# One attention-and-mixers kernel: how the first head pair is loaded, rounded and marked, and who copies six PSUM tiles of the first three periods

## The chip, the cores and the metric

The kernel runs on one core of one Trainium2 chip. The metric is device time in microseconds (us) of one execution, in which the kernel reads everything from HBM, computes and writes its output back. The engines are named as in the profile: PE (TensorE, matrix products), PEld (its weight loads), DVE (VectorE), ACT (ScalarE), POOL (GpSimd) and SP (SyncE, which here only starts transfers). Each engine works through its own list of instructions in order and waits for the others by semaphores.

## What is computed

Three layers follow each other. The first is an attention whose mask is a hash: each query and each key gets six sign bits by a projection, and a query sees only the keys with the same six bits. The other two are mixers of large matrix products. Cut to what matters:

```python
q_bits = einsum('bhsd,dk->bhsk', q, proj) > 0     # q, k, v: batch 2, 8 heads, 768 rows, 64 columns
k_bits = einsum('bhsd,dk->bhsk', k, proj) > 0     # proj: 64 x 6
mask   = bucket(q_bits)[..., None] == bucket(k_bits)[..., None, :]
scores = where(mask, q @ k.T / 8, -1e9)
attn   = softmax(scores) @ v                      # then (2, 768, 512)
x      = sigmoid(xr @ w_r) * (relu(xk @ w_k)**2 @ w_v)     # xk, xr: mixes of x and the row before it
u, v   = split(relu(x @ w_in)); v = normalise(v)
out    = (u * (w_spatial @ v + b_spatial)) @ w_out
```

Products are formed from rounded parts: a float32 value is split into a rounded high part and the remainder, the low part, and the low parts are multiplied too.

## The kernel before

The 16 heads are worked on as eight pairs, and each pair as 24 units: a unit is one block of 128 queries of one head against all 768 keys. Three units make a period, so there are 64 periods (`p` in the loop at L518), eight per pair. The units of a pair run over the first half of its queries for head `e` = 0, then for `e` = 1, then over the second half in the same way. So period 0 is head 0, period 1 is head 1, period 2 is head 0 again.

For each head there is one operand tile `TK` of 128 partitions by four slots of 768 columns. One half of the partitions, `lo_rows`, holds the rounded k in slot 0, the low part of k in slot 1, the rounded q in slot 2 and the low part of q in slot 3. The other half, `hi_rows`, holds the rounded k in slot 0, the rounded q in slot 3, and in slots 1 and 2 zeros with twelve rows of scaled sign bits, which make the mask. The scores of a unit (`scores`, L316) are two products with two column halves each, four matmuls: slot 3 against slot 0, then slot 2 against slot 1. The second pair of matmuls therefore needs the bits and the low part of k, and the first needs the low part of q.

A unit then goes through these steps: `peak` (L332) is one pass of DVE that copies the scores out of PSUM and finds their maximum; `bias` is a small scaling on DVE; `expo` (L347) is the exponential on ACT; `transp` (L359) makes six PE transposes in two halves into PSUM tiles `t`; `evac` (L367) copies each half out into `PT` on ACT; and three periods later `av` (L397) multiplies by v. There are two PSUM tiles for scores and three for `t`. So a period has six evictions, all on ACT.

The preparation of a pair has these steps. `load_x` (L236) brings q and k, in float32, into the tile `raw`, of which there is one buffer: the pool has `bufs=1` and each pair takes the tag "x" again, so the load of the next pair waits for the last reader of this one. `load_pair` (L241) brings the rounded parts into `TK` by four transfers from POOL's queue that round on the way. `bits_mm` (L271) is four products of `raw` with the projection, into a `t` tile called `z`; `bits_sign` (L280, DVE) makes the tile `zb` of signs, `bits_scale` (L287) the scaled tile `zc`, and `bits_place` (L292) brings its rows to `TK` by eight small transfers on SP's queue, or, for the first head of the first pair, four by copies on DVE and ACT. `split_part` and `split_piece` (L254 to L263) subtract the rounded part from `raw` to get the low parts.

Jobs of a period are kept in a table `plan` with two places per period: place 0 is after the exponential of the second unit, place 1 at the end of the period. Place 0 of period 0 holds the load of `raw` for pair 1 and `load_pair(1)`; place 0 of period 1 holds `bits_mm(1)`, `bits_sign(1)` and `bits_scale(1)`; periods 1 and 2 hold the eight pieces of the low parts of pair 1 on POOL; and from period 2 on weight conversions run on DVE (L44, L49 and others), with `recip` (L377) in every second period.

Ahead of the loop stands the prologue, L483 to L505, in which the first pair is prepared. `warm` (L265) is a run of PE products on nothing, 12 ahead of the first bits and 8 behind them, each of which shows as two passes in the trace.

Of the kernel before, what the change touches and what calls it, by code (L numbers as in the profile page):

```python
# [10 lines left out]
F32 = mybir.dt.float32  # L11
F32R = mybir.dt.float32r
AF = mybir.ActivationFunctionType
ALU = mybir.AluOpType
AX = mybir.AxisListType

B, H, S, D = 2, 8, 768, 64
NP = H // 2
HS = S // 2
# [1 line left out]
DF = 1024  # L21
NB = 6
BIG = float(2 ** 30)
WARM_A, WARM_B = 12, 8
U32 = mybir.dt.uint32
W_MIN = float(np.array([0x38000000], np.uint32).view(np.float32)[0])
W_MAX = float(np.array([0x47EFFFFF], np.uint32).view(np.float32)[0])
# [55 lines left out]
def hash_attention_moe_kernel(  # L83
# [134 lines left out]
    with tc.manual_schedule():  # L218
        attention(**env)
        mixers(**env)  # L220


def attention(tc, nc, mid, dram, ident, msc, omu, misc, cst_sb, pb, epsT, kq, vP, XT, TK0, wr, w_r, wk,
              w_k, w_v, ps_s, ps_t, obank, mix_jobs, r_group, tick, now, at_tick, plan_weight, wv, **_):
    PS = bass.MemoryType.PSUM
    with ExitStack() as ctx:
        at = ctx.enter_context(tc.tile_pool(name="at", bufs=1))

        TK = [TK0, [at.tile([128, 4, S], F32R, name=f"tk1_{e}") for e in range(2)]]
        lo_rows = {0: slice(64, 128), 1: slice(0, 64)}  # L230
        hi_rows = {0: slice(0, 64), 1: slice(64, 128)}

        raw, vt = {}, {}
        npairs = B * NP

        def load_x(pp):  # L236
            b, p = divmod(pp, NP)
            raw[pp] = mid.tile([128, 2, S], F32, tag="x", name="x")
            (nc.gpsimd if pp > 1 else nc.sync).dma_start(raw[pp], kq[b, p].rearrange("t r s -> r t s"))

        def load_pair(pp):  # L241
            b, p = divmod(pp, NP)
            for e in range(2):
                src = kq[b, p][:, 64 * (1 - e):64 * (1 - e) + 64].rearrange("t d s -> d t s")
                t = TK[pp % 2][e]
                nc.gpsimd.dma_start(t[lo_rows[e], 0:3:2, :], src)
                nc.gpsimd.dma_start(t[hi_rows[e], 0:4:3, :], src)

        def load_v(pp):
            b, p = divmod(pp, NP)  # L250
            vt[pp] = at.tile([128, 6, 2, D], F32, tag="v", bufs=2, name="v")
            nc.sync.dma_start(vt[pp], vP[b, p])
# [7 lines left out]
        def split_part(pp, e, n, eng):  # L260
            l = lo_rows[e]
            t = TK[pp % 2][e]
            eng.tensor_sub(t[l, 1 + 2 * n, :], raw[pp][l, n], t[l, 2 * n, :])  # L263

        def warm(n):  # L265
            for _ in range(n):
                nc.tensor.matmul(obank[:, :128], ident, ident, start=True, stop=True)

        zs = {}

        def bits_mm(pp):  # L271
            zs[pp] = ps_t.tile([128, 512], F32, tag="t", name="z")
            for g in range(4):
                o = (g % 2) * HS
                nc.tensor.matmul(
                    zs[pp][32 * g:32 * g + 32, :HS], pb, raw[pp][:, 1 - g // 2, o:o + HS],
                    start=True, stop=True,
                )

        def bits_sign(pp):  # L280
            zb = at.tile([128, HS], F32, tag="zb", name="zb")
            nc.vector.tensor_scalar(
                zb, zs[pp][:, :HS], 0.0, cst_sb[:, 0:1], op0=ALU.is_gt, op1=ALU.subtract
            )
            zs[pp] = zb

        def bits_scale(pp, eng):  # L287
            zc = at.tile([128, HS], F32R, tag="zc", name="zc")
            eng.tensor_scalar(zc, zs[pp], cst_sb[:, 1:2], None, op0=ALU.mult)
            zs[pp] = zc  # L290

        def bits_place(pp, first=False):  # L292
            zc = zs.pop(pp)
            for e in range(2):
                for g in range(4):
                    o = (g % 2) * HS
                    a0 = 64 * e
                    s0 = 32 * g + 12 * e
                    dst = TK[pp % 2][e][a0:a0 + 12, 2 - g // 2, o:o + HS]
                    src = zc[s0:s0 + 12, :].bitcast(F32)  # L300
                    if first and e == 0:
                        if g % 2:
                            nc.vector.tensor_copy(dst, src)
                        else:
                            nc.scalar.copy(dst, src)
                    else:
                        nc.sync.dma_start(dst.bitcast(F32), src)

        def clear(r, eng):
            for e in range(2):  # L310
                eng.memset(TK[r][e][hi_rows[e], 1:3, :].bitcast(F32), 0.0)
# [4 lines left out]
        def scores(i):  # L316
            g, u = divmod(i, 6)
            pp, half = divmod(g, 2)
            e, j = divmod(u, 3)
            t = TK[pp % 2][e]  # L320
            q0 = half * HS + 128 * j
            s = ps_s.tile([128, 2, 512], F32, tag="s", name="s")
            for n in range(2):
                w = t[:, 3 - n, q0:q0 + 128]
                for c in range(2):
                    nc.tensor.matmul(  # L326
                        s[:, c, :HS], w, t[:, n, c * HS:(c + 1) * HS],
                        start=(n == 0), stop=(n == 1),
                    )
            S_ps[i] = s  # L330

        def peak(i):  # L332
            s = S_ps.pop(i)
            c = at.tile([128, 2, HS], F32, tag="p", bufs=3, name="p")
            m = at.tile([128, 1], F32, tag="m", bufs=4, name="m")
            nc.vector.tensor_scalar(  # L336
                c, s[:, :, :HS], -BIG / 2, None, op0=ALU.max, op1=ALU.max, accum_out=m
            )
            C_sb[i] = (c, m)

        def bias(i):
            c, m = C_sb[i]
            nb = at.tile([128, 1], F32, tag="nb", bufs=4, name="nb")
            nc.vector.tensor_scalar(nb, m, -0.125, None, op0=ALU.mult)  # L344
            C_sb[i] = (c, nb)
# [13 lines left out]
        def transp(i, c):  # L359
            p = P[i] if c == 0 else P.pop(i)  # L360
            t = ps_t.tile([128, 512], F32, tag="t", name="t")
            for n in range(3):
                k0 = 128 * (3 * c + n)
                nc.tensor.transpose(t[:, 128 * n:128 * n + 128], p[:, k0:k0 + 128], ident)  # L364
            return t

        def evac(i, c, t):  # L367
            g, u = divmod(i, 6)
            e, j = divmod(u, 3)
            nc.scalar.copy(  # L370
                PT[g][:, e, 3 * c:3 * c + 3, 128 * j:128 * j + 128],
                t[:, :HS].rearrange("p (n q) -> p n q", n=3),
            )
# [43 lines left out]
        plan = {}  # L417
# [3 lines left out]
        def at_slot(p, k, job):  # L421
            plan.setdefault((p, k), []).append(job)
# [58 lines left out]
                at_slot(max(p0 + 3, 0), 0, lambda n=pp + 2: load_x(n))  # L481

        nc.scalar.dma_start(msc, misc)  # L483
        nc.vector.memset(ident, 0.0)
        load_x(0)
        load_pair(0)
        clear(0, nc.vector)
        warm(WARM_A)
        split_part(0, 0, 1, nc.gpsimd)
        split_part(0, 0, 0, nc.vector)  # L490
        bits_mm(0)
        bits_sign(0)
        bits_scale(0, nc.vector)
        bits_place(0, True)
        warm(WARM_B)
        for r in rcs:
            nc.vector.memset(r, 0.0)
        split_part(0, 1, 0, nc.vector)
        split_part(0, 1, 1, nc.gpsimd)
        make_identity(nc, ident)  # L500
        load_v(0)
        nc.gpsimd.memset(XT[:, :, :, 0:1], 0.0)
        nc.gpsimd.memset(epsT, 1e-6)
        nc.gpsimd.tensor_scalar(omu, msc[:, 34:42], -1.0, 1.0, op0=ALU.mult, op1=ALU.add)
        clear(1, nc.gpsimd)  # L505

        def av3(p):
            for n in range(3):
                av(p // 2, 3 * (p % 2) + n)

        def move(i, c):
            evac(i, c, transp(i, c))

        def score(i):
            peak(i)
            bias(i)

        for p in range(np3):  # L518
            a = 3 * p
            scores(a)  # L520
            scores(a + 1)
            score(a)
            if a:
                move(a - 1, 0)
            expo(a)
            if a:
                move(a - 1, 1)
            score(a + 1)
            expo(a + 1)
            if p >= 3:  # L530
                av3(p - 3)
            if p >= 2 and p % 2 == 0:
                recip(p // 2 - 1)
            for job in plan.pop((p, 0), ()):
                job()
            if p >= 3 and p % 2:
                spread((p - 3) // 2)
            if p >= np3 - 2:
                tick()
            scores(a + 2)  # L540
            move(a, 0)
            move(a, 1)
            score(a + 2)
            expo(a + 2)
            if p >= 4 and p % 2 == 0:
                finish((p - 4) // 2)
            move(a + 1, 0)
            move(a + 1, 1)
            for job in plan.pop((p, 1), ()):
                job()  # L550
            if p == np3 - 2:
                plan_wv()
            if p >= np3 - 2:
                tick()
# [322 lines left out]
```

## Time and profile before

| | us |
|---|---|
| median of 3 runs | 560.82 |
| lowest and highest | 560.57, 561.64 |
| span of the profiled execution | 557.4 |
| PE busy in it | 543.7 |
| first matmul of the scores starts | 10.27 |
| `bits_mm` of pair 1 starts | 19.25 |

The profiled execution's span runs from its first to its last instruction. The median lies 3.4 us above it, which is what lies around the instructions. PE is busy for 98% of the span and is the bound from the middle of the first pair on. The stretch that concerns the change is the first 32 us, in which PE is not yet full.

### The profile page before, as it was taken

How to read it: one execution, taken by the hardware profiler on the slowest of the kernel's cores; microseconds unless marked ns; L12 is line 12 of the kernel's file. 1: busy time of each engine (PE TensorE's matmuls, PEld its weight loads, DVE VectorE, ACT ScalarE, POOL GpSimd, SP SyncE). 2: the span in 40 equal slices, each digit the busy share in tenths (PEclk: the TensorE clock that was granted, in tenths of full speed). 3: DMA queues.
4: the chain of work that ended last, by engine and by line, in shares of the span. 5: the costliest groups of instructions: out<-in, count | busy, mean ns of one | idle time of the engine just before them, and what ended most of it. 6: DMA issues, size and time to landing. Idle time of an engine off the chain costs nothing.

```text
span 557.4 us, 9008 instructions
## 1 busy us (share of the span) xinstructions
PE 543.7 (98%) x3188; PEld 465.8 (84%) x3188; DVE 381.4 (68%) x812; ACT 335.4 (60%) x718; POOL 146.4 (26%) x152
## 2 busy tenths in 40 slices
PE   7899999999999999999999999999999999999997
PEld 6767676767676767789999999999998989899896
DVE  6778888888888889558796676316997784443230
ACT  1978888888888879849743856519345443221211
POOL 5774858585858533200000000000110000000000
PEclk9999999999999999999999999999999999999999
DMA  8957494859585710210031211000672100001102
GB/s 175 274 173 150 139 173 147 169 135 180 152 162 167 150 48 16 88 56 7 32 114 39 61 53 39 0 1 2 197 227 85 58 29 2 1 19 39 56 20 95
DMA packets 20477, 51.96 MB, mean 93 GB/s; under 512 B 3840, under 2 KB 6864, under 8 KB 20432
## 3 DMA queue, kind: packets, MB, share of 16 engines
q1 hardware_dynamic: 13664, 31.44, 18.3%
q0 software_dynamic: 6336, 19.66, 17.6%
q8 instruction: 25, 0.41, 0.3%
q10 hardware_dynamic: 432, 0.28, 0.2%
q14 instruction: 20, 0.16, 0.1%
HBM read 47.08 MB, written 3.19 MB: 90 GB/s over the span
## 4 chain that ended last, share of the span: by engine, by line
PE 78%; DVE 13%; ACT 5%; issue 2%; DMA 1%; DVEq 0%; ACTq 0%; POOLq 0%
PE o L176 11%; PE v L631 9%; PE o L399 9%; PE t L364 9%; PE s L326 8%; PE k L176 8%; PE s L176 7%; PE w L176 5%; PE u L176 5%; DVE p L336 5%; PE o L631 3%; PE r L176 3%; ACT p L354 2%; DVE w_a L49 2%; DVE w_a L44 2%
## 5 line engine op out<-in xcount | busy, mean ns | idle before, releaser
L336 DVE TENSOR_SCALAR_CACHE_REDUCE p<-s 128x768 f32<-128x768 f32 x96 | 91.7, 956 | 22.3 <-PE s L326 20.4
L354 ACT ACTIVATE p<-p,nb 128x768 f32<-128x768 f32 x96 | 90.8, 946 | 16.0 <-DVE nb L344 15.4
L370 ACT COPY PT<-t 128x384 f32<-128x384 f32 x192 | 84.1, 476 | 19.3 <-PE t L364 18.5
L326 PE MATMUL s<-tk 128*128 128x384 f32 x384 | 87.1, 360 | 3.8 <-DVE p L336 1.7
L326 PEld LDWEIGHTS s<-tk 128*128 128x128 f32 x384 | 64.7, 191 | 25.0 <-issue 6.7
L364 PE MATMUL t<-ident,p 128*128 128x128 f32 x576 | 78.7, 277 | 3.8 <-ACT p L354 3.8
L364 PEld LDWEIGHTS t<-ident,p 128*128 128x128 f32 x576 | 65.4, 141 | 14.3 <-ACT p L354 7.2
L399 PE MATMUL o<-PT,v 128*64 128x384 f32 x384 | 68.8, 494 | 0.0
L258 POOL TENSOR_TENSOR tk<-x,tk 64x384 fp32r<-64x384 f32 x56 | 62.4, 1138 | 3.4 <-issue 2.0
L176 PE MATMUL k<-tk,wk 128*128 128x384 f32 x336 | 59.6, 334 | 0.0
L176 PEld LDWEIGHTS k<-tk,wk 128*128 128x128 f32 x336 | 58.4, 188 | 0.0
L631 PE MATMUL v<-k,wv 128*128 128x384 f32 x288 | 53.6, 334 | 0.0
L631 PEld LDWEIGHTS v<-k,wv 128*128 128x128 f32 x288 | 50.3, 188 | 0.0
L399 PEld LDWEIGHTS o<-PT,v 128*64 128x64 f32 x384 | 24.8, 136 | 28.5 <-issue 27.5
L690 POOL DMA_DIRECT2D wsp<-in_w_spT_dram x6 | 3.6, 615 | 167.7 <-DVE w_a L44 161.3
L176 PE MATMUL o<-wk,tk 128*128 128x512 f32 (+1 forms) x168 | 36.2, 374 | 0.0
L176 PEld LDWEIGHTS o<-wk,tk 128*128 128x128 f32 x168 | 30.0, 188 | 5.5
L612 ACT ACTIVATE kr<-k 128x384 f32<-128x384 f32 x28 | 13.6, 487 | 31.2 <-PE k L176 31.0
L176 PE MATMUL r<-tk,wr 128*128 128x384 f32 x168 | 30.9, 337 | 0.2 <-DVE tk L122 0.2
L121 ACT CAST tk<-g 128x384 fp32r<-128x384 f32 x16 | 8.2, 514 | 37.5 <-DVE g L761 37.5
L176 PE MATMUL w<-wk,tk 128*128 128x512 f32 x132 | 30.7, 390 | 0.0
L176 PEld LDWEIGHTS r<-tk,wr 128*128 128x128 f32 x168 | 29.0, 188 | 1.8 <-ACT PT L370 0.6
(108 smaller groups left out, 858.6 us busy)
## 6 DMA issues: line engine op xcount, KB each, us to landing
tk<-in_kq_dram POOLq DMA_DIRECT2D x32, 384.0 KB, 9.6
x<-in_kq_dram POOLq DMA_DIRECT2D x6, 768.0 KB, 4.9
w_raw<-in_w_k_dram SPq DMA_DIRECT2D x8, 512.0 KB
w_raw<-in_w_v_dram SPq DMA_DIRECT2D x8, 512.0 KB
w_raw<-in_w_in_dram SPq DMA_DIRECT2D x8, 512.0 KB
v<-in_vP_dram SPq DMA_DIRECT2D x8, 384.0 KB
rb<-ds SPq DMA_DIRECT2D x32, 96.0 KB
out_dram<-ot SPq DMA_DIRECT2D x11, 256.0 KB
```

What stands on the lines that cost most here:

```text
L44: nc.vector.tensor_scalar(st["a"].bitcast(F32), st["a"].bitcast(F32), W_MIN, W_MAX, op0=ALU.max, op1=ALU.min)
L49: nc.vector.tensor_scalar(st["a"], st["a"], 3, 0x3FFFFFFF, op0=ALU.logical_shift_left, op1=ALU.bitwise_and)
L176: nc.tensor.matmul(o, a, x, start=(i == 0), stop=(i == len(seq) - 1))
L258: nc.gpsimd.tensor_sub(tk[l, 1 + 2 * t, o], raw[pp][l, t, o], tk[l, 2 * t, o])
L326: nc.tensor.matmul(s[:, c, :HS], w, t[:, n, c * HS:(c + 1) * HS], start=(n == 0), stop=(n == 1),)
L336: nc.vector.tensor_scalar(c, s[:, :, :HS], -BIG / 2, None, op0=ALU.max, op1=ALU.max, accum_out=m)
L354: nc.scalar.activation(c, c, AF.Exp, bias=nb, scale=0.125, accum_out=den[g][:, u:u + 1])
L364: nc.tensor.transpose(t[:, 128 * n:128 * n + 128], p[:, k0:k0 + 128], ident)
L370: nc.scalar.copy(PT[g][:, e, 3 * c:3 * c + 3, 128 * j:128 * j + 128], t[:, :HS].rearrange("p (n q) -> p n q", n=3),)
L399: nc.tensor.matmul(obank[64 * e:64 * e + 64, :HS], vt[g // 2][:, kt, e, :], PT[g][:, e, kt, :], start=(kt == 0), stop=(kt == 5),)
L612: nc.scalar.activation(r, o[:, :HS], AF.Relu)
L631: nc.tensor.matmul(os[m][:, :HS], w, x, start=(c == 0 and k == 0), stop=(c == 7 and k == 2),)
```

## The change

The first pair's `raw` is loaded in two halves, first k and then q, both on SP's queue. The rounded parts of its first head no longer come by transfer: `first_head` copies them out of `raw` on DVE and ACT, and `first_low` makes the low part of q in halves on POOL. The transfers from POOL's queue are left for the second head only. The bits of the first head are scaled as they are copied to their place, three copies on DVE and one on ACT, out of `zb`; the scaled tile `zc` is still made, now on POOL and for the second head only. The identity is made at the very start on POOL, the zeros of the second head's tile are now set by POOL, the low part of k of the second head moves into place 0 of period 0 (on DVE), and the zeros of the second set of tiles move to place 1 of period 0. The warm-up is 7 and 4 products instead of 12 and 8. In periods 0 to 2 DVE takes two of the six evictions: the second halves of the first two units of the period.

```diff
-WARM_A, WARM_B = 12, 8
+WARM_A, WARM_B = 7, 4
...
+        def load_halves(pp):
+            b, p = divmod(pp, NP)
+            raw[pp] = mid.tile([128, 2, S], F32, tag="x", name="x")
+            for t in range(2):
+                nc.sync.dma_start(raw[pp][:, t, :], kq[b, p, t])
...
+        def first_head():
+            x, t = raw[0], TK[0][0]
+            lo, hi = lo_rows[0], hi_rows[0]
+            nc.vector.tensor_copy(t[lo, 0, :], x[lo, 0])
+            nc.scalar.copy(t[hi, 0, :], x[lo, 0])
+            nc.vector.tensor_sub(t[lo, 1, :], x[lo, 0], t[lo, 0, :])
+            for n in range(2):
+                o = slice(n * HS, n * HS + HS)
+                nc.scalar.copy(t[lo, 2, o], x[lo, 1, o])
+            nc.vector.tensor_copy(t[hi, 3, :], x[lo, 1])
+
+        def first_low(e, n):
+            l, o = lo_rows[e], slice(n * HS, n * HS + HS)
+            t = TK[0][e]
+            nc.gpsimd.tensor_sub(t[l, 3, o], raw[0][l, 1, o], t[l, 2, o])
+
+        def first_places():
+            for g in (2, 3, 0, 1):
+                dst, s0 = place_at(0, 0, g)
+                src, by = zs[0][s0:s0 + 12, :], cst_sb[s0:s0 + 12, 1:2]
+                if g == 3:
+                    nc.scalar.mul(dst, src, by)
+                else:
+                    nc.vector.tensor_scalar(dst, src, by, None, op0=ALU.mult)
...
         nc.scalar.dma_start(msc, misc)
-        nc.vector.memset(ident, 0.0)
-        load_x(0)
-        load_pair(0)
-        clear(0, nc.vector)
+        load_halves(0)
+        make_identity(nc, ident)
+        load_pair(0, (1,))
+        nc.vector.memset(TK[0][0][hi_rows[0], 1:3, :].bitcast(F32), 0.0)
+        nc.gpsimd.memset(TK[0][1][hi_rows[1], 1:3, :].bitcast(F32), 0.0)
         warm(WARM_A)
-        split_part(0, 0, 1, nc.gpsimd)
-        split_part(0, 0, 0, nc.vector)
+        first_head()
+        first_low(0, 0)
         bits_mm(0)
         bits_sign(0)
-        bits_scale(0, nc.vector)
-        bits_place(0, True)
+        first_places()
         warm(WARM_B)
+        bits_scale(0, nc.gpsimd)
+        bits_place(0, (1,), (2, 3, 0, 1))
+        first_low(1, 0)
+        first_low(0, 1)
+        first_low(1, 1)
         for r in rcs:
             nc.vector.memset(r, 0.0)
-        split_part(0, 1, 0, nc.vector)
-        split_part(0, 1, 1, nc.gpsimd)
-        make_identity(nc, ident)
         load_v(0)
...
-        clear(1, nc.gpsimd)
+        plan.setdefault((0, 0), []).insert(0, lambda: split_part(0, 1, 0, nc.vector))
+        at_slot(0, 1, lambda: clear(1, nc.gpsimd))
...
             move(a, 0)
-            move(a, 1)
-            score(a + 2)
+            if p < 3:
+                t = transp(a, 1)
+                score(a + 2)
+                evac(a, 1, t, nc.vector.tensor_copy)
+            else:
+                move(a, 1)
+                score(a + 2)
...
-            move(a + 1, 1)
+            move(a + 1, 1, nc.vector.tensor_copy if p < 3 else nc.scalar.copy)
```

## Rows read from the trace of the kernel before

**Rows 1.** The page: span; busy us of each engine; one group (busy, mean ns, idle).
```profile
span 557.4 us, 9008 instructions
PE 543.7 (98%) x3188; PEld 465.8 (84%) x3188; DVE 381.4 (68%) x812; ACT 335.4 (60%) x718; POOL 146.4 (26%) x152
...
L370 ACT COPY PT<-t 128x384 f32<-128x384 f32 x192 | 84.1, 476 | 19.3 <-PE t L364 18.5
```
**Rows 2.** The chain that ended last, first 24 us: start, length, what.
```profile
1.24 6.33 DMA tk<-in_kq_dram
...
11.55 2.18 PE s L326 x6
...
19.25 0.85 PE z L275 x8
...
23.27 0.98 DVE p L336 x2
```
**Rows 3.** Timeline of PE: start, length, what, idle time before and its releaser.
```profile
6.02 0.85 PE L275 MATMUL z<-x,msc 128*32 128x384 f32 x8 [0.20 <-DMA x<-in_kq_dram]
...
18.20 0.82 PE L364 MATMUL t<-ident,p 128*128 128x128 f32 x6
```
**Rows 4.** Timeline of SP: the transfers it starts.
```profile
10.46 3.19 SPq L307 DMA_DIRECT2D tk<-zc  x4
13.70 0.51 SPq L252 DMA_DIRECT2D v<-in_vP_dram  x1
14.40 0.39 SPq L239 DMA_DIRECT2D x<-in_kq_dram  x1
```
**Rows 5.** Tile x: time from issue to landing of its loads.
```profile
DMA to landing us min/median/max: 4.7/4.9/5.3
```
**Rows 6.** Timeline of DVE and POOL, 7 to 12 and 26 to 28 us.
```profile
7.65 2.57 POOL L263 TENSOR_TENSOR tk<-x,tk 64x768 fp32r<-64x768 f32 x1 [3.84 <-DMA tk<-in_kq_dram]
8.58 0.62 DVE L282 TENSOR_SCALAR zb<-z,msc 128x384 f32<-128x384 f32 x1
9.24 1.20 DVE L289 TENSOR_SCALAR zc<-zb,msc 128x384 fp32r<-128x384 f32 x1
12.48 0.96 DVE L336 TENSOR_SCALAR_CACHE_REDUCE p<-s 128x768 f32<-128x768 f32 x1 [0.23 <-PE s L326]
27.55 1.12 DVE L49 TENSOR_SCALAR w_a<-w_a 128x512 uint32<-128x512 uint32 x1
```
**Rows 7.** Single source lines over the run: duration ns minimum, median, maximum.
```profile
L49 DVE TENSOR_SCALAR w_a<-w_a x32: 426/428/1118, 27.5 to 419.7; 128x512 uint32<-128x512 uint32 x32
L258 POOL TENSOR_TENSOR tk<-x,tk x56: 991/1012/1542, 24.3 to 199.1; 64x384 fp32r<-64x384 f32 x56
L289 POOL TENSOR_SCALAR zc<-zb,msc x7: 1239/1241/1246, 21.0 to 187.3; 128x384 fp32r<-128x384 f32 x7
L303 DVE CAST tk<-zc x2: 348/350/351, 10.5 to 10.8; 12x384 fp32r<-12x384 f32 x2
L305 ACT CAST tk<-zc x2: 508/510/513, 10.5 to 11.0; 12x384 fp32r<-12x384 f32 x2
L263 DVE TENSOR_TENSOR tk<-x,tk x2: 952/954/955, 7.6 to 11.3; 64x768 fp32r<-64x768 f32 x2
L411 DVE TENSOR_TENSOR XT<-o,rb x16: 557/558/559, 42.4 to 240.4; 128x384 f32<-128x384 f32 x16
```
**Rows 8.** Stretches: length, busy of PE, PEld, DVE, ACT, POOL, clock, DMA share, GB/s.
```profile
8.85:11.55 2.70, 0.62 (x3) 0.30 (x2) 2.59 (x7) 1.02 (x2) 1.60 (x2) 1.00 1.27 211
25.00:30.00 5.00, 3.16 (x20) 2.28 (x19) 4.83 (x12) 3.24 (x9) 4.93 (x6) 1.00 0.94 152
```
**Rows 9.** PE by stretches: length, busy (instructions), granted clock, DMA share, GB/s.
```profile
11.50:12.00 0.50, 0.45 (x2) 0.72 0.48 71
12.00:12.50 0.50, 0.50 (x3) 0.50 0.12 28
...
15.00:16.00 1.00, 0.86 (x7) 0.94 0.91 246
```

More of the change, by code (lines that the diff above doesn't have):

```diff
@@ L239, in load_x, with load_pair @@
             (nc.gpsimd if pp > 1 else nc.sync).dma_start(raw[pp], kq[b, p].rearrange("t r s -> r t s"))
-        def load_pair(pp):
+        def load_halves(pp):
             b, p = divmod(pp, NP)
-            for e in range(2):
+            raw[pp] = mid.tile([128, 2, S], F32, tag="x", name="x")
+            for t in range(2):
+                nc.sync.dma_start(raw[pp][:, t, :], kq[b, p, t])
+        def load_pair(pp, es=(0, 1)):
+            b, p = divmod(pp, NP)
+            for e in es:
                 src = kq[b, p][:, 64 * (1 - e):64 * (1 - e) + 64].rearrange("t d s -> d t s")
@@ L290, in bits_scale, with place_at, bits_place @@
             zs[pp] = zc
-        def bits_place(pp, first=False):
+        def place_at(pp, e, g):
+            o = (g % 2) * HS
+            return TK[pp % 2][e][64 * e:64 * e + 12, 2 - g // 2, o:o + HS], 32 * g + 12 * e
+        def bits_place(pp, es=(0, 1), gs=(0, 1, 2, 3)):
             zc = zs.pop(pp)
[L294 to L307, printed above, removed]
+            for e in es:
+                for g in gs:
+                    dst, s0 = place_at(pp, e, g)
+                    nc.sync.dma_start(dst.bitcast(F32), zc[s0:s0 + 12, :].bitcast(F32))
+        def first_head():
[20 more added lines that the diff above has]
+                    nc.vector.tensor_scalar(dst, src, by, None, op0=ALU.mult)
         def clear(r, eng):
@@ L365, in transp, with evac @@
             return t
-        def evac(i, c, t):
+        def evac(i, c, t, copy=nc.scalar.copy):
             g, u = divmod(i, 6)
             e, j = divmod(u, 3)
-            nc.scalar.copy(
+            copy(
                 PT[g][:, e, 3 * c:3 * c + 3, 128 * j:128 * j + 128],
@@ L509, in av3, with move @@
                 av(p // 2, 3 * (p % 2) + n)
-        def move(i, c):
-            evac(i, c, transp(i, c))
+        def move(i, c, copy=nc.scalar.copy):
+            evac(i, c, transp(i, c), copy)
         def score(i):
```

## The prediction

> **What bounds the kernel now.** The page comes first: PE is busy for 543.7 of 557.4 us [rows 1], so whatever is won has to be won where PE isn't full, and that is the start. The chain of waits says where: until 7.57 us it is the rounding transfers of the first pair, then DVE's preparation of the bits, and the first scores that count start at 11.55 [rows 2]. This view tempts the reader to take the whole stretch ahead of 11.55 for the prize. The second thing to see in it is the PE product of the bits of pair 1, `z` at 19.25, from which PE works through without a gap until 23.27, where DVE takes over [rows 2]. PE takes its work in order, so `z` is a gate: all that lies ahead of it matters only as far as it lets `z` start sooner. The timeline of PE shows its last work ahead of the gate ending at 19.02 [rows 3], so PE stood hardly at all there. The timeline of SP then shows what else the gate needs: `raw` of pair 1, whose load is started at 14.40, right behind that of v [rows 4]. The time from issue to landing of such loads is 4.7 to 5.3 us [rows 5]; the product at 19.25 shows that this one had landed 4.85 us after its issue at the latest. So the load was nearly as late as PE was. It is the question of this case: does the change start that load sooner?
>
> **The first head, up to its bits.** In the kernel before, `raw` of pair 0 landed at 6.0 us, seen by the product that waited for it [rows 3]. The change sends the same 768 KB on the same queue in two parts. The k part comes sooner, and hides the copying of k (1.02 us on ACT at the most, twice 0.51 for 384 columns [rows 7]) and the subtraction (0.95 us on DVE [rows 7]) behind the wait for q. The q part ends when the whole did, or a little sooner, since two of four rounding transfers are gone: 5.3 to 6.0, I take 5.85. Then the bits: product 0.85 us [rows 3], to 6.70, signs 0.62 [rows 6], to 7.35. Before, the signs ended at 9.20 [rows 6], so the head start here is 1.85 us. The shorter warm-up may leave that product at the lower clock, which could cost up to its own length, 0.85 us, once.
>
> **What follows goes one by one.** The timeline of DVE and POOL shows a second thing. The scaling of the bits on DVE started at 9.24 and took 1.20 us; POOL's subtraction ran from 7.65 to 10.22 [rows 6], and DVE was done 0.22 us behind its end. A weight shift takes 0.43 us when nothing is beside it, and 1.12 where it stands between two of POOL's subtractions [rows 6, 7]. The signs, which DVE reads out of PSUM, took 0.62 beside the same POOL operation [rows 6], no more than elsewhere. So as these rows show it, a DVE operation that has all its operands in SBUF waits for the POOL operation under way, and the next takes its turn behind another one of POOL's. The change puts just such operations side by side. From the end of the signs at 7.35 there are: the rest of POOL's first low part (it can start once ACT has copied the first half of q, 0.51 us after 5.85, or behind DVE's copy of q; rest 0 to 0.55, I take 0.3); three placing copies on DVE, 0.35 each [rows 7]; POOL's scaling for the second head, 1.24; three low parts on POOL, 1.01 each; and DVE's subtraction for the second head, 0.95 [rows 7]. Sum 0.3 + 1.05 + 1.24 + 3.03 + 0.95 = 6.57. Whoever goes first, the last ends at 7.35 + 6.57 = 13.92, with small gaps about 14.05; without any wait for one another POOL alone would need 0.3 + 1.24 + 3.03 = 4.57, to 11.9, and DVE's subtraction, which stands behind two peaks of 0.98 us and their small followers [rows 2], would end about 12.2 to 13. The rows are nearer to the first case, since both engines would be working without a break.
>
> The Trainium skill has a rule for it (SBUF — State Buffer, section "SBUF: two separate sides"): VectorE and GpSimd share a pair of ports as an exclusive lock, held for a whole instruction. It speaks against putting the scaling and the low parts on POOL here. The rows agree with it, with the 1.12 for 0.43 us above.
>
> **The gate.** `raw` has one buffer, and its last readers are exactly the last of that list: the third of POOL's low parts and DVE's subtraction, which the change moves behind the second unit's peak. SP is free for the load earlier (four small transfers take 3.19 us [rows 4] from the end of the scaling at 9.3 to 10, and the load of v 0.51), at 13.1 to 13.8. So the load of pair 1's `raw` starts at about 14.05, against 14.40 before: the head start of 1.85 us has shrunk to 0.35. The rounding transfers of pair 1 now start ahead of it instead of 3 us behind it, and share the way; the first load of the kernel had such company and took the 5.3 us, the others 4.7 to 4.9 [rows 5]. On the other side v no longer fills the way right ahead of it. I take 4.85 as before, bounds 4.7 and 5.3. The gate then opens at 18.9, with bounds 18.4 and 19.4, against 19.25: a gain of 0.35 us, between a gain of 0.85 and a loss of 0.15.
>
> All else of periods 0 and 1 is done by then: the first peak starts at about 10.8 instead of 12.48 [rows 6] because DVE's placing copies stand ahead of it, and two further peaks, the moved subtraction and the transposes end at about 17.2. The four small transfers of the second head's bits are behind `zc`, at 9.3 to 10, plus 3.19 and a landing of some 2 us: 15, early enough for a gate at 18.9. PE would stand still for 1.7 us ahead of the gate.
>
> **The evictions.** Twice in a period ACT is spared 0.48 us [rows 1], 0.95 in all, and DVE gets two copies out of PSUM, about 0.56 each by the nearest row of that shape [rows 7], 1.1 us. In periods 0 and 1 neither is on the path, since the gate is; that cover gone, ACT's 0.95 us a period would be a gain. Behind the gate, in period 2, DVE is busy for 4.83 of 5.0 us [rows 8], and the copies come behind the third unit's peak there; the next exponentials are ACT's, which has lost as much. So nothing in the sum, at most 1.1 us lost. Also in period 2, the waits of DVE for POOL (0.7 us in the weight shift alone) may fall otherwise than before, by 0.4 us to either side.
>
> **The sum.** 0.35 us off the profiled execution's span of 557.4, so 557.0 to 557.1; the median shown is 560.82, 3.4 above the span, and 560.82 - 0.35 is about 560.4. PE is full from there on, so this stays to the end.
>
> **Rivals.** First, *the head start survives*. Nothing of the 1.85 us would be lost if the loads are quicker in less company or if POOL and DVE pass each other: the load of pair 1 then starts at 13.1, when SP is free, and lands 4.7 us later, at 17.8, a gain of 1.45; with the first q half landing at 5.3, the early bound, up to 2.0. It gives 558.8 to 559.4, in the middle 559.2. Against it are the sum of turns above and the one buffer. The Trainium skill speaks for it (DMA: Bandwidth & Descriptors, section "Anatomy of one DMA — SWDGE (gpsimd) path"): it fits 2.0 us plus the bytes at 436 GB/s, an estimate of 3.8 us for 768 KB. The trace has 4.7 to 5.3 for such loads [rows 5] and so disagrees; by the fit the gate would open at 17.9 instead of 18.9, and the time be 559.4.
>
> Second, on the slower side: *PE's clock falls while PE stands at the gate*. Between 8.85 and 11.55 us PE was busy for 0.62 of 2.70 us, and then its granted clock fell from 2.4 to 1.2 GHz (0.72 in the stretch from 11.5, 0.50 from 12.0) and was back at about 15.1 [rows 8, 9]. With 3.16 of 5.0 us busy it stayed up [rows 8]. In the changed kernel PE stands still for some 1.7 us, up to 2.5, with sparse work ahead of it. A fall that begins at the gate takes half of 3.4 us, 1.7 us, of which some 0.2 would lie behind the stretch in which PE is the path: +1.5 - 0.35, about 562.0. [...]
>
> Third, *DVE becomes the bound of period 2*: the whole 1.1 us of copies lands on the path, 560.82 - 0.35 + 1.1 = 561.6.
>
> Fourth, the halves *don't do what they say*: both land together at 6.0 and the copies of k follow one another then, 1.0 to 1.5 us later than I have it. The load of pair 1 then goes out at about 14.9, and the time is 561.0 to 561.7.
>
> **How the numbers follow.** My forecast, the head start eaten by the turns at the port and the one buffer, has 0.45 and its own range 559.8 to 561.2. The surviving head start has 0.26, the fallen clock 0.17, DVE's period 0.06, the halves 0.06. A measurement of this kernel can tell about 0.2% (1.1 us) from no change. Faster by more than that, under 559.7: 0.26 and a little from the forecast's edge, 0.28. Slower, over 561.9: most of the clock's 0.17 and a share of the last two, 0.20. Within: 0.52. The range reaches down to 558.7, nearly all of the first rival, and up to 562.4, past the clock's price.
>
> **What would show it.** Right: the load of pair 1's `raw` starts within half a us of 14.0, its last release is DVE's moved subtraction or POOL's third low part, and PE waits for that DMA at `z` with 1 to 2.5 us idle; placing copies and the subtraction on DVE are longer than 0.35 and 0.95 where POOL works. Wrong: `z` starts ahead of 18, or PE's wait ahead of it is not for the load, or the granted clock reads 0.50 between 19 and 23 us.

## The result and the profile after

| | before | after |
|---|---|---|
| median, us | 560.70 (4 runs) | 564.72 (4 runs) |
| lowest and highest | 560.56, 561.64 | 563.78, 566.17 |
| ratio of the times | | 1.0073, 95% interval 1.0053 to 1.0094 |
| span of the profiled execution | 557.4 | 564.4 |

The changed kernel is slower by 0.7%, about 4.0 us. The forecast was 560.4, no change, with a range up to 562.4: the time lies outside it, on the side that had a chance of 0.20.

The profiled execution of after took 566.17 us, the slowest of its four, so its trace shows a loss of 7.0 us of span where the medians show 4.0. It is good for where the time went, and less for how much. The execution's time lies 1.8 us above its span, and so it does in each kernel below. By that the profiled execution of before took some 559.2 us; the rest of the 3.4 us that stands ahead of the prediction was the scatter between one execution and the median. A few executions of the kernels below took far longer, 585 to 1878 us: the ratios leave them out, and since the profiled ones of e1, e6 and a2 are among them, only the times of these three are used.

The chain that ended last, after, first 41 us (start, length, what):

```profile
0.74 3.03 DMA x<-in_kq_dram
3.79 0.86 DVE tk L312
...
5.66 1.25 DVE tk L318
6.94 0.63 DVE zb L288
7.59 0.41 DVE tk L332
8.01 0.64 DVE tk L332
8.69 0.65 DVE tk L332
...
11.65 1.53 DVE tk L269
...
13.38 10.18 DMA x<-in_kq_dram
...
23.70 1.51 PE z L281 x8
25.21 1.58 PE s L351 x4
26.79 2.56 PE t L389 x12
29.35 0.83 PE s L351 x4
...
30.30 0.98 DVE p L361 x2
...
38.91 2.09 PE o L424 x12
```

One line stands out: the load of pair 1's `raw`, 10.18 us long, where the same load of before had landed 4.85 us after its start at the latest [rows 2, 4]. The gate `z` opens at 23.70 instead of 19.25 [rows 2], 4.45 us late. From there to the peak of DVE it takes 30.30 - 23.70 = 6.60 us, against 23.27 - 19.25 = 4.02 [rows 2]: another 2.58. The two together, 7.03, are all of the 7.0 by which the span grew.

The timeline of PE around the gate (start, length, what, idle time before and its releaser):

```profile
15.35 0.87 PE L389 MATMUL t<-ident,p 128*128 128x128 f32 x6 [0.27 <-ACT p L379]
23.70 1.51 PE L281 MATMUL z<-x,msc 128*32 128x384 f32 x8 [7.48 <-DMA x<-in_kq_dram]
```

PE stands for 7.48 us. The same eight passes take 1.51 us, not 0.85 [rows 3]: PE comes back at the lower clock. By stretches of PE, after (length, busy and instructions, granted clock, DMA share, GB/s):

```profile
18.00:20.00 2.00, 0.00 (x0) 0.81 1.18 283
20.00:22.00 2.00, 0.00 (x0) 0.50 1.26 279
24.00:26.00 2.00, 2.00 (x11) 0.50 1.28 263
28.00:30.00 2.00, 2.00 (x11) 0.63 0.41 95
```

The granted clock falls from 2.4 to 1.2 GHz while PE stands, and is only on its way back from 28 to 30, with PE full. Why the load is late is seen where two queues are laid side by side; SP's and POOL's, after:

```profile
9.15 3.20 SPq L307 DMA_DIRECT2D tk<-zc  x4
12.39 0.51 SPq L258 DMA_DIRECT2D v<-in_vP_dram  x1
13.38 0.39 SPq L239 DMA_DIRECT2D x<-in_kq_dram  x1
...
13.17 0.69 POOL L252 DMA_DIRECT2D tk<-in_kq_dram  x1
13.86 0.61 POOL L253 DMA_DIRECT2D tk<-in_kq_dram  x1
```

The first of the four rounding transfers (L252) starts 0.21 us ahead of the load. In before it started 3.0 us behind it. Less is moved then, too: the same two stretches, first of before, then of after (length, granted clock, DMA share, GB/s).

```profile
16.00:18.00 2.00, 1.00 1.01 387
18.00:20.00 2.00, 1.00 1.03 420
```

```profile
16.00:18.00 2.00, 1.00 1.03 274
18.00:20.00 2.00, 0.81 1.18 283
```

In before all of it went over SP's queue there, the rounding transfers having moved nothing yet. In after the two queues share the stretch; queue by queue, from 18 to 20 us (`q1` is SP's queue, `q0` POOL's; packets, MB, share of the DMA engines' time):

```profile
q1 hardware_dynamic: 98, 0.31, 68.5%
q0 software_dynamic: 99, 0.26, 49.3%
```

### The profile page after: what moved, and what is told of

Same layout as the page of the kernel before. It is cut to its first block, busy times and chain, and to the rows that moved or that the text cites. A ratio compares the mean times of both kernels' runs of the same rounds, so it can differ in the third digit from the quotient of the medians.

```text
span 564.4 us, 8978 instructions
## 1 busy us (share of the span) xinstructions
PE 543.2 (96%) x3170; PEld 463.9 (82%) x3170; DVE 384.4 (68%) x818; ACT 334.8 (59%) x714; POOL 147.3 (26%) x154
## 4 chain that ended last, share of the span: by engine, by line
PE 77%; DVE 13%; ACT 5%; DMA 3%; issue 1%; DVEq 0%; ACTq 0%; SPq 0%
PE o L176 11%; PE v L664 9%; PE o L424 9%; PE t L389 9%; PE k L176 8%; PE s L351 8%; PE s L176 7%; PE w L176 5%; PE u L176 5%; DVE p L361 5%; PE o L664 3%; PE r L176 3%; DMA x<-in_kq_dram 2%; DVE w_a L49 2%; ACT p L379 1%
## 5 line engine op out<-in xcount | busy, mean ns | idle before, releaser
L395 ACT COPY PT<-t 128x384 f32<-128x384 f32 x186 | 81.9, 476 | 29.4 <-PE t L389 28.3
L389 PE MATMUL t<-ident,p 128*128 128x128 f32 x576 | 80.0, 280 | 4.0 <-ACT p L379 3.9
```

The costliest lines, as they stand in the source:

```text
L395: copy(PT[g][:, e, 3 * c:3 * c + 3, 128 * j:128 * j + 128], t[:, :HS].rearrange("p (n q) -> p n q", n=3),)
```

## The experiments

The theory after the result: the load is late because the rounding transfers of pair 1, which no longer wait for two fills on POOL (`clear(1)`, which the change moved behind them), run beside it; that makes the gate late, and the clock falls on top. Rivals: what stands on the load's own queue (v ahead of it, two weight loads behind it), the evictions on DVE, the clock alone, the halves. Later the first theory split in two: is it the company of the rounding transfers, or who starts first?

**e1 and e1b, the zeros ahead again** (the same kernel twice).

```diff
-        at_slot(0, 1, lambda: clear(1, nc.gpsimd))
+        clear(1, nc.gpsimd)
```

> The changed kernel with one part undone: the zeros of the second set of tiles (2.8 us on POOL) stand in the prologue again, ahead of the four rounding transfers of pair 1, which so start at about 16 us instead of 13.2. Theory A (these transfers, started just ahead of the load of pair 1's raw, take its way, and it lands 10.2 us after its issue instead of 4.85): the load, issued at 13.4, lands at about 18.3 to 18.8, the product of the bits starts there instead of at 23.7, and the time falls to 559 to 560. Rival B (the load is slow because of v and two weight loads on its own queue, or because of the shorter gap to the first loads): the product stays at 23 to 24 and the time at 564 to 566.

> The same kernel as the run with the zeros first, once more, for a trace with PE at its clock: the four rounding transfers of pair 1 start at about 16 us, the load of pair 1's raw at 13.4. Theory A (company on the way): this load lands 5 to 6 us after its issue, and the product of the bits starts at 18.3 to 19.5, PE having waited 2 to 3 us. Rival B (the load is slow for a reason of its own queue): it starts at 23 to 24. Time 560.5 to 562.

Measured: 561.5 us, ratio 1.0019 (1.0005 to 1.0033), and 560.6, ratio 0.9996 (0.9973 to 1.0020). From e1b's chain:

```profile
13.36 6.08 DMA x<-in_kq_dram
19.57 0.85 PE z L281 x8
```

With the rounding transfers 2.5 us behind (from 15.89) the same load, started at the same time and with the same neighbours on its own queue, lands in 6.08 instead of 10.18. This one line of the change, the place of the zeros, makes nearly all of the loss. What is left is no change, as forecast (e1's 561.5 lies over the 559 to 560 that I had expected of it).

**e3, the same move alone, in the kernel before.**

```diff
-        clear(1, nc.gpsimd)
+        at_slot(0, 1, lambda: clear(1, nc.gpsimd))
```

> The kernel before with one line moved: the zeros of the second set of tiles (2.8 us on POOL) go behind the four rounding transfers of pair 1, which so start at about 14.6 us instead of 17.4, right beside the load of pair 1's raw at 14.4. Theory A (company on the way): the load lands 8 to 10 us after its issue, the product of the bits starts at 22.5 to 24.5 instead of 19.25, and the kernel is slower by 3 to 6 us, 564 to 567. Rival B (what made the load late in the changed kernel is something else in its prologue): no change, 560 to 561.5.

Measured: 562.74 us, ratio 1.0029 (1.0008 to 1.0050); its times fall in two groups, 558.6 to 560.9 and 562.5 to 564.4, and the profiled one is of the second. Its chain:

```profile
14.40 8.24 DMA x<-in_kq_dram
...
22.78 0.85 PE z L275 x8
```

The rounding transfers start at 14.21, 0.19 us ahead of the load, and `z` comes 3.5 us later than in before. So the lateness needs nothing else of the change, though here it strikes only some of the executions, and the loss, 0.3%, is less than I had expected (564 to 567 us).

**a2, the changed kernel again, unaltered.**

> The changed kernel itself once more, beside the other three. The load of pair 1's raw is expected to land 9 to 11 us after its issue again and the product of its bits to start at 22.5 to 24.5; time 563.5 to 566.5.

Measured: 565.12 us, ratio 1.0081 (1.0063 to 1.0099): the loss is there again, at the same size.

**e4, all evictions on ACT in the changed kernel, and e6, DVE's evictions in the kernel before.** In e4 `evac` is called without `nc.vector.tensor_copy` and stands ahead of `score(a + 2)` again; e6 is the reverse edit.

> The changed kernel with all six evictions on ACT again. As in the prediction, the two copies a period on DVE lie beside the path: within 0.4 us of the changed kernel, 564 to 566. Rival: they bind DVE in period 2, and giving them back gains up to 1.1 us, 563 to 564.5.

> The kernel before with only the evictions of the change: DVE takes two of six in periods 0 to 2. As in the prediction they lie beside the path there too, PE being the chain from 16 to 23 us: 560 to 561.5, no change. Rival (DVE is the bound of period 2): slower by up to 1.1 us, 561.5 to 562.

Measured: e4 565.01 us, ratio 1.0087 (1.0068 to 1.0106), as the changed kernel; e6 561.05, ratio 1.0001 (0.9978 to 1.0024). The evictions move nothing either way.

**e7, the first load whole.**

```diff
-        load_halves(0)
+        load_x(0)
```

> The changed kernel with the first pair's raw in one load again, everything else as changed. The halves let the copies and the subtraction of k start at 3.8 instead of about 5 us. Without them the signs of the bits end about 0.5 to 1 us later, the moved subtraction and with it the load of pair 1 go out later by as much, 13.9 to 14.4, and the time is 0.5 to 1 us above the changed kernel, 564.5 to 566; if the halves do nothing, no change.

Measured: 567.83 us, ratio 1.0124 (1.0088 to 1.0160). Its chain:

```profile
0.74 4.47 DMA x<-in_kq_dram
...
14.50 10.30 DMA x<-in_kq_dram
...
24.94 1.50 PE z L281 x8
```

The load of pair 1 starts 1.12 us later and is as slow, 10.30. So the halves do what they say, and are worth 1.2 us at the gate; the medians say 3, more than I had expected (564.5 to 566 us), and the rest is left open.

**e2 and e2b, PE kept busy ahead of the gate** (the same kernel twice): 24 products on nothing ahead of `bits_mm(1)`.

```diff
+                if pp == 0:
+                    at_slot(1, 0, lambda: warm(24))
```

> The changed kernel with 24 idle products (48 passes of about 0.12 us, 5.8 us) for PE ahead of the bits of pair 1, where it stood still for 7.5 us. Nothing else changes. If the fallen clock is a cost of its own (23.70 to 30.30 us took 6.60, the same work 4.02 in the kernel before), the granted clock stays at 2.4 GHz, the load still lands at 23.5, the same stretch takes about 4.0, and the time is about 562.5 to 564. If the late load is all of the loss, nothing changes: 564 to 566.

> The kernel with 24 idle products ahead of the bits of pair 1, once more, since its six times spread over 5 us. If the clock that falls at the gate is a cost of its own, it is 1 to 2.5 us faster than the changed kernel timed beside it and its mean granted clock is nearer to 1. If not, the two are within 0.7 us of each other.

Measured: 565.33 us, ratio 1.0092 (1.0065 to 1.0120), and 564.82, ratio 1.0074 (1.0053 to 1.0094). The timeline of PE, and in e2 one row of DVE's below it, first e2, then e2b:

```profile
16.16 5.52 PE L273 MATMUL o<-ident 128*128 128x128 f32 x48
23.91 0.85 PE L281 MATMUL z<-x,msc 128*32 128x384 f32 x8 [2.23 <-DMA x<-in_kq_dram]
...
27.94 0.96 DVE L361 TENSOR_SCALAR_CACHE_REDUCE p<-s 128x768 f32<-128x768 f32 x1
```

```profile
16.16 5.52 PE L273 MATMUL o<-ident 128*128 128x128 f32 x48
23.78 1.23 PE L281 MATMUL z<-x,msc 128*32 128x384 f32 x8 [2.10 <-DMA x<-in_kq_dram]
```

With the same 5.52 us of work and some 2.2 us of standing behind it, the clock held in the one execution (DVE's peak at 27.94, 4.03 us behind `z`, as in before) and fell in the other. So the trace prices the clock at 6.60 - 4.03 = 2.6 us, but the medians gained nothing. What the clock costs in the median is left open. That it isn't the loss by itself is seen below: in the traces of e8 and e13 too the granted clock was 0.50 from 20 to 22 us, and e8 is faster than before, e13 slower by 0.2%.

**e5, the load started early, into a place of its own; e9, the same in the kernel before.** `raw` of pair 1 is put into the tile `XT`, unused at that time, so that it needn't wait for the readers of pair 0's, and ACT starts the load right behind the bits of the first head.

```diff
+            if pp == 1:
+                raw[1] = XT[:, 0:2, 1, 1:1 + S]
+                nc.scalar.dma_start(raw[1], kq[b, p].rearrange("t r s -> r t s"))
+                return
...
-            if pp + 2 < npairs:
+            if 0 <= pp < npairs - 2:
                 at_slot(max(p0 + 3, 0), 0, lambda n=pp + 2: load_x(n))
...
         first_places()
+        load_x(1)
```

> The changed kernel with the one buffer and the company taken away: raw of pair 1 gets a place of its own (a part of the tile XT that is written only from period 36 on), and its load is started by ACT at about 8.3 us, where ACT stands idle and the transfers of pair 0 have ended. If the late landing and the clock that falls behind it are all of the loss, the load lands at about 13 to 14, the product of the bits of pair 1 starts at about 16.3 instead of 23.7, right behind PE's work, and the stretch behind it takes 4.0 us at 2.4 GHz: 7.4 + 2.6 us off the profiled execution, about 3 us under the kernel before, 556.5 to 558.5. If something else in the changed start holds PE too (the moved subtraction, the bits of the second head, the copies on DVE), the gain over the kernel before is under 1 us: 559.5 to 561.

> The kernel before with raw of pair 1 in the tile XT and its load started by ACT at about 11.5 us, behind the copies of the bits, instead of 14.4. In its trace PE had its own work until 19.02 and the bits of pair 1 at 19.25, so an earlier load can win 0.2 us there: 559.5 to 561. That would make the 5 us of the same measure in the changed kernel the worth of the changed start once the gate is open. If the load alone is what that measure gains, this kernel gains 3 us or more too: 557.5 or less.

Measured: e5 554.98 us (554.38 to 555.46), ratio 0.9901 (0.9865 to 0.9937), faster than both kernels; e9 560.44, ratio 0.9993 (0.9979 to 1.0007). The timeline of PE in e5, and below it two rows of its DVE:

```profile
15.34 0.88 PE L393 MATMUL t<-ident,p 128*128 128x128 f32 x6 [0.28 <-ACT p L383]
16.15 0.85 PE L285 MATMUL z<-XT,msc 128*32 128x384 f32 x8
...
23.16 0.38 DVE L44 TENSOR_SCALAR w_a<-w_a 128x512 f32<-128x512 f32 x1
23.58 0.43 DVE L49 TENSOR_SCALAR w_a<-w_a 128x512 uint32<-128x512 uint32 x1
```

`z` follows PE's own work without a wait at 16.15. In e9 it starts at 19.32, as in before: there PE was the gate, not the load. So with the change PE comes to the gate 3.2 us sooner; its gain is there once the load of pair 1 no longer eats it. e5 gains more than I had expected (556.5 to 558.5 us). Of the 4.8 us between the spans of before and e5, 3.1 are there at `z`; the rest fits period 2, where POOL starts its pieces only at 23.75 and DVE's rows are unheld (0.43 in L49 for 1.12 [rows 6]), but no run tests that.

**e8, the place of its own alone, the load left on SP in its place.** The diff is the first part of e5's, with `nc.sync` for `nc.scalar`.

> The changed kernel with a place of its own for raw of pair 1 (in the tile XT), its load still in its old place on SP's queue, behind v and with the rounding transfers of pair 1 starting at 13.2. This takes away the wait for the one buffer and leaves the company. If the company is the cause, the load goes out at 12.9 instead of 13.4 and lands 9 to 10 us later all the same, the product of the bits starts at 22 to 23.5, and the time is at most 1.5 us under the changed kernel's. If the one buffer is the cause (as the prediction's gate had it), it lands at 17.5 to 18.5 and the time is 557 to 559.5.

Measured: 557.93 us, ratio 0.9960 (0.9941 to 0.9979). Its chain:

```profile
12.95 5.17 DMA XT<-in_kq_dram
18.26 0.85 PE z L285 x8
```

Of the two outcomes set against each other, lateness by company failed; time and landing are those given for the one buffer. Without the wait for pair 0's readers the load starts 0.43 us sooner, the rounding transfers (13.18) are issued where they were, and it lands in half the time. The order of start is turned round. Place and order are still mixed here; e11 parts them.

**e10 to e13, the order of start set on purpose.** e10 does the operation on `omu` (L531) twice, e12 and e13 put a quarter and a half of pair 1's zeros ahead of the rounding transfers, so that these start later; e11 puts `load_pair(1)` of e8 three small POOL operations sooner.

```diff
         nc.gpsimd.tensor_scalar(omu, msc[:, 34:42], -1.0, 1.0, op0=ALU.mult, op1=ALU.add)
+        nc.gpsimd.tensor_scalar(omu, msc[:, 34:42], -1.0, 1.0, op0=ALU.mult, op1=ALU.add)
...
-        at_slot(0, 1, lambda: clear(1, nc.gpsimd))
+        nc.gpsimd.memset(TK[1][0][hi_rows[0], 1:3, :].bitcast(F32), 0.0)
+        at_slot(0, 1, lambda: nc.gpsimd.memset(TK[1][1][hi_rows[1], 1:3, :].bitcast(F32), 0.0))
...
-                at_slot(p0, 0, lambda n=pp + 1: load_pair(n))
+                if pp:
+                    at_slot(p0, 0, lambda n=pp + 1: load_pair(n))
...
+        load_pair(1)
         nc.gpsimd.memset(XT[:, :, :, 0:1], 0.0)
```

(The first part is e10's. The second is e13's; e12 has `1:2` in the first fill and the rest in the place. The last two are e11's, on top of e8's.)

> The changed kernel with one tiny operation of POOL (omu, 128 x 8) issued twice, so that the rounding transfers of pair 1 start some 0.8 us later, at about 14.0 instead of 13.17, and so behind the load of pair 1's raw, which is started at 13.38, instead of 0.21 us ahead of it. If the order of start decides: the load lands in 5 to 6 us instead of 10.18, the product of the bits starts at 18.5 to 20.0 instead of 23.70, and the kernel takes 558 to 561.5 us. If it is the rounding transfers' company that makes the load late, whichever starts first: still 8.5 to 10 us of landing, the product at 22 to 23.5, and 563 to 565 us.

> The changed kernel with pair 1's raw in a place of its own and its load left on SP, as in e8, and the four rounding transfers of pair 1 put three tiny POOL operations earlier, at about 12.3 instead of 13.18, so that they start some 0.6 us ahead of the load at about 12.95 instead of 0.23 behind it. If the order of start decides: the load takes 9 to 11 us instead of 5.17, the product of the bits starts at 22 to 24 instead of 18.26, and the kernel takes 562 to 565.5 us. If the own place is what made the load quick in e8: 5 to 6 us again, the product at 18 to 19, and 556.5 to 559.5 us.

> The changed kernel with a quarter of pair 1's zeros (one 64 x 768 fill on POOL, some 0.7 us) put back ahead of its rounding transfers: these start at about 13.9, the load of pair 1's raw still at 13.4, so 0.5 us ahead of them instead of 0.2 behind (0.06 ahead in e10, which landed in 10.01). If a lead of the load decides: landing in 5 to 6.5 us instead of 10.18, the product of the bits at 18.8 to 20.3 instead of 23.70, 558.5 to 562 us. If the company of the rounding transfers as such decides, by how much of the load lies beside them: nearly all of it still does, landing 9 to 10 us, the product at 22.5 to 23.5, 563 to 565.5 us.

> The same with half of pair 1's zeros (two such fills, 1.43 us) ahead: the rounding transfers start at about 14.6, 1.2 us behind the load. If a lead decides: landing in 5 to 6.2 us, the product at 18.8 to 19.8, 558.5 to 561.5 us. If the company as such decides: between the 10.18 of the changed kernel and the 6.08 of e1b, where the lead was 2.5 us, so 8 to 8.5 us, the product at 21.5 to 22, 562 to 563.5 us.

Measured, by the lead of the load over the first rounding transfer in the profiled execution; the fifth column is what POOL's queue, on which only the rounding transfers stand, moved between the start of the load and its landing:

| kernel | load starts | lead, us | lands in | rounding moved, MB | `z` at | median, us |
|---|---|---|---|---|---|---|
| e11 (own place) | 13.07 | -0.64 | 8.62 | 0.88 | 21.82 | 562.89 |
| after | 13.38 | -0.21 | 10.18 | 0.92 | 23.70 | 564.72 |
| e3 (before) | 14.40 | -0.19 | 8.24 | 0.70 | 22.78 | 562.74 |
| e7 | 14.50 | -0.16 | 10.30 | 0.85 | 24.94 | 567.83 |
| e10 | 12.71 | +0.06 | 10.01 | 0.79 | 22.85 | 565.65 |
| e8 (own place) | 12.95 | +0.23 | 5.17 | 0.15 | 18.26 | 557.93 |
| e12 | 13.44 | +0.46 | 7.04 | 0.29 | 20.61 | 564.66 |
| e13 | 13.81 | +1.11 | 5.90 | 0.03 | 19.85 | 560.68 |
| e1b | 13.36 | +2.53 | 6.08 | none | 19.57 | 560.60 |

The leads of e2, e2b and e4 are those of after, -0.21 and -0.22, and their loads land in 10.16 to 10.29.

The rows for e11, e12 and e13, in this order, from their chains:

```profile
13.07 8.62 DMA XT<-in_kq_dram
```

```profile
13.44 7.04 DMA x<-in_kq_dram
```

```profile
13.81 5.90 DMA x<-in_kq_dram
```

e11 against e8 settles the place: in its own place too the load is slow once it starts behind, 8.62 for 5.17, and 562.89 us (ratio 1.0046, 1.0032 to 1.0060) for 557.93. e13, with 1.1 us of lead, lands in 5.90, where I had wanted 8 or more if the company as such decides. Its ratio is 1.0024 (1.0003 to 1.0046). But that expectation took the company from the times of issue. The fifth column shows that in e13 there was hardly any: 0.03 MB of the rounding transfers moved before the load had landed. All that moved between the start of the load and its landing, first after, then e1b, queue by queue:

```profile
DMA packets 866, 2.57 MB, mean 252 GB/s; under 512 B 68, under 2 KB 68, under 8 KB 866
q1 hardware_dynamic: 535, 1.65, 66.4%
q0 software_dynamic: 331, 0.92, 36.7%
```

```profile
DMA packets 543, 1.67 MB, mean 275 GB/s; under 512 B 39, under 2 KB 39, under 8 KB 543
q1 hardware_dynamic: 543, 1.67, 89.3%
```

SP's queue moved the same in both: the load's 0.79 MB, at most 0.39 of v, and so 0.47 or more of the two weight loads behind it. The total rate is nearly the same too. What after has besides is 0.92 MB of the rounding transfers, 3.7 us at its 252 GB/s, of the 4.1 us by which its load is later. So it is their company after all, and who starts first settles whether there is any.

e10 missed its aim: the second `omu` operation took 0.2 us and not the 0.8 of the first, the load itself went out at 12.71, the lead became 0.06 us, and the load was as slow as behind (565.65 us, ratio 1.0093, 1.0077 to 1.0110). e12 lies between: 7.04 in its profiled execution, which was its fastest (561.6), and a median of 564.66 (ratio 1.0075, 1.0054 to 1.0096) that says that most of its executions took longer. So the change from late to quick falls in the first half us or so of lead, and isn't sharp there; the leads of executions that weren't profiled are not known. That e11's load into `XT` is quicker by 1.5 us than that of after, with nearly as much beside it, is left open.

## Why the prediction was wrong

- *PE's gate is the product of the bits of pair 1, and the load of its `raw` decides it*: right. PE waits for that DMA and nothing else (7.48 us in after).
- *The head start*: the signs ended at 7.56, forecast 7.35. By another way than told: q was there by 4.96, sooner than the 5.85 that I took, but the signs stood behind DVE's copy of q (L318), which took 1.25 us beside a subtraction of POOL.
- *Turns at the port and the one buffer*: the buffer right, the turns in part. DVE's placing copies took 0.41 to 0.65 where I had taken 0.35, its moved subtraction 1.53 for 0.95 [rows 7], and that subtraction was the last reader for which the load waited. POOL was hardly held: its scaling and three low parts ran from 7.73 to 12.35, 4.62 us for a sum of 4.27. So the turns took 13.16 - 7.56 = 5.6 us and not the full sum of 6.57, nearer to the case that I had set aside (12.2 to 13). Forecast start 14.05, measured 13.38, against 14.40 before: a little outside the half us around 14.0 that was set as the mark, on the good side. Here the rule of the Trainium skill (SBUF — State Buffer, section "SBUF: two separate sides") and the rows agree again, with that 1.53 for 0.95.
- *The landing, "I take 4.85 as before, bounds 4.7 and 5.3"*: this is the step that failed. It measured 10.18. I had seen that the rounding transfers would now start ahead of the load, and priced that company by "the first load of the kernel" and its 5.3 us [rows 5]. That was a misreading. The landings of rows 5 are those of the six loads that POOL's queue starts, and the 5.3 belongs to the first of these, at 32.71, ahead of the next rounding transfers (38.07). From 32 to 39 us of before (KB, us to landing):

```profile
x<-in_kq_dram POOLq DMA_DIRECT2D x1, 768.0 KB, 5.3
```

  The kernel's first load, by the product that waited for it, took at most 6.02 - 0.74 = 5.28 us [rows 3], but it had started half a us ahead of its rounding transfers (first at 1.24 [rows 2]), and 0.35 MB of these moved by 6.0. No row of before showed a load behind rounding transfers. From what was to move, 0.79 MB for the load and 1.57 MB for the four rounding transfers, the 387 to 420 GB/s of before give some 6 us. That lies over the bound of 5.3, and still far from 10.18, since the rate in after was 252 and the weight loads shared the way too. What the runs showed in place of 4.85: 0.92 MB of rounding beside the load, worth 4.1 us (after against e1b).
- *PE stands still 1.7 us*, and *the clock falls at the gate* (a rival, 0.17): with the late load it stood 7.48 us, and the clock did fall (0.50 from 20 us on, one of the signs that the prediction had named for being wrong), at 2.6 us in the trace instead of the 1.7 of the rival. It followed the late load: the price was worked out for a short wait. e2 shows that it can be kept up, and not that this wins time.
- *The evictions cost nothing*: right (e4 and e6). *DVE as the bound of period 2* would have shown as a gain in e4 or a loss in e6: neither is there. *The halves do nothing*: no, 1.2 us at the gate (e7).
- *The head start survives* (a rival, 0.26): not in this kernel, but e5 shows what it was worth with the load out of the way, more than I gave it: 1% or 5.5 us, since PE's own work ended at 16.2.
- *What lies around the span*: 1.8 us, not 3.4. The sum itself used only the difference, so nothing followed from it.

Had the load landed as quickly as in e1b, the time would have stayed in the range: e1b and e1 took 560.6 and 561.5 us. The gain at the gate would not have come even so, since 6.08 us is still over the bound of 5.3: `z` started at 19.57 there, against a forecast of 18.9 and 19.25 before.

## What to carry to other kernels

The time from issue to landing that a trace shows belongs to the neighbours that the transfer had there: when a change moves a transfer, or only moves something that another queue waited behind, list every transfer that will start within a few us of it, on all queues, and see whose start comes first; afterwards count what each queue moved while the transfer was under way, since the times of issue alone don't show who had company. A fill that looks idle can be holding a neighbour's transfers back; moving it is a change to the load that everybody waits for. And a gain at the head of a kernel is worth something only if the load behind the next gate is freed with it, by a place of its own and an earlier start: alone either of the two brought nothing or lost here (after, e9), together they brought 1%.

## What the runs showed of the hardware

A load of 768 KB from SP's queue, issued near four rounding transfers of 384 KB each from POOL's queue, landed, in the profiled executions, in 8.2 to 10.3 us where it started behind the first of them or within 0.1 us ahead, in 7.0 with a lead of 0.46 us (e12, most of whose executions took longer), and in 5.2 to 6.1 with a lead of 1.1 us or more and, into another tile, of 0.23 (e8). In the late cases the rounding transfers moved 0.70 to 0.92 MB meanwhile, in the quick ones 0.15 at the most.

The Trainium skill (DMA: Bandwidth & Descriptors, section "Queues, rings and completion order") says that each DMA engine takes turns between its queues packet by packet. The rows of after agree: from 18 to 20 us it has 98 packets of SP's queue and 99 of POOL's. What no run here shows is why a small lead keeps the rounding transfers back for so long: issued at 13.17 and 13.18, they moved 0.10 MB from 16 to 17 us in after and one packet in e8, where the load had started 0.43 us sooner.
